# A fused attention and gated convolution: another table of issue order, engines and store queues

## The chip, the core and the metric

The kernel runs on one core of a Trainium2 chip. A core has TensorE (PE: matmuls and transposes, results into PSUM), VectorE (DVE), ScalarE (ACT) and GpSimd (POOL), each with its own queue that it works through in order, and SyncE (SP), which here only issues DMAs. DMAs can be issued by SP, ACT and POOL. PSUM has eight banks of 128 partitions x 512 fp32 values. The metric is the time of one execution on the device in microseconds (us); less is better.

## The reference

Two softmax attentions with 32 packed queries between them, then a gate whose middle factor is a circular convolution along the sequence:

```python
def sm_attn(qq, kk, vv):
    a = softmax(qq @ kk.T / sqrt(64)); return a @ vv
p_packed = sm_attn(p, k, v)                  # 32 x 64 for each of 8 x 8 heads
x = sm_attn(q, p_packed, p_packed)           # 576 x 64 for each, heads side by side: 8 x 576 x 512
x1, x2, x3 = split(x @ w_proj)               # each 8 x 576 x 512
x2 = irfft(rfft(x2, axis=1) * rfft(filter))  # along the 576 places
out = (x1 * x2 * x3) @ w_out                 # 8 x 576 x 512, fp32
```

## The kernel before, in words

The eight batches go one after the other through four stages, and the stages of neighbouring batches lie side by side in time. `front(b)` turns p, k and q (on PE, or by a DMA transpose where `TURNED` or `KEYS` names the batch), makes the first softmax with its sums on PE (`pv`), its reciprocal on DVE (`rz`), the packed values, their transpose, its copies into a block tile (`ppk`), the scores of the second softmax and its probabilities `a`. `turn(b)` projects the packed values with `wp` (`qm`), brings the probabilities to the frequency domain (`fa`, by way of `ez`) and turns them (`a2t`). `middle(b)` multiplies five spectra with the filter's (`tt`, `gm`, on DVE and POOL) and makes the gate x1 * x3 in four quarters and a rest (`w`; a copy of x1 out of PSUM, then a multiplication by x3). `back(b)` makes the inverse transform (`y`, `yt`) and the product with `wout`, copies it on ACT into the same quarters of `w` (or into `os`), and stores it: six stores a batch, eight where the rest of two batches goes with it.

Buffers: two each of k, v, q (`kn`, `vn`, `qn`; even and odd batches) and of `w`. So batch b + 2 can be loaded when PE has read batch b, and batch b + 2's gate copy into a quarter of `w` waits until batch b's store out of that quarter has landed.

Nothing of the order on the engines is set by the program's text. A recorder (`Recorder`) takes down every operation in the order of the text, with the engines that could do it (`either`), and then `emit` issues them in the order of a table, with the engine and the PSUM bank that the table names, each tied to the one before it on its engine. The table is `TABLE`, three numbers for each operation and one for each PSUM tile, packed. Since all operations are issued from one line of `emit`, the trace gives the same line, L193, for all; tiles tell them apart.

All loads of p, k, q, v, `wp` and `wout` are issued by POOL, between its arithmetic. The stores go through `send`, which lets the table choose SP or ACT. The DMA transposes are SP's.

Last, `spin(n)` records n matmuls of 256 columns on a tile of zeros, whose results are not read. The table places them among PE's work: 59, of which 39 stand ahead of the first real matmul.

Of the kernel before, what the change touches and what calls it, by code (L numbers as in the profile page):

```python
# [18 lines left out]
P = 128  # L19
# [29 lines left out]
def _constants(S):  # L49
# [34 lines left out]


TABLE = (
    'c-qaD30zdw8o=+pbMK5x;8TfQMiEUgL(NLfEtQ^<h+FtGOM0nKd%2eQs+Y~&1=j$>P*cOSMGec;lw8QALJ1_rB|*((kr)LH(3hA#@qOnz=g!<2%pBbM&'
    'vLi3eEWB!@8hqD*XoP4e6CsAT?@JLuwdq|1_xgZ;;&q2)vBW9?}5Oj7A;y_2q2to?xL(2q10-1R5WRFzNpmi?5X0@CrcbzCBDbXYZuijIC7*Z;)~=g%S'
    '}IVp#0#%!(yGRL;Ke3Z-|s2KD+m17VpVL(&{tz&#XkYto|(@IgCtNb+nj~QC9Y1Ou@Miel-wp8*;S7O9u5j-QN+ha(GdnzWq-PEzBF7H0b!ifr}#|p3G'
    '$&Wn9>=@0|_oE!_7&_IJUVK|yDc-KD^Gy5{DFryDeAkY0c1hI$2rpDMQD@!0zH8`lBHzF=goUHcOuGxInh=5S$Q&Mqg3IiF=_#*9TK%p8RDK~h$RA(6e'  # L90
    'dZcR<?^XSpmJ9eZz7`Sm`z{<3=W{Veh-mrXm(!yTI+O<6?pD*sqSnw$NubI6b(wgBrMVil;FyYN;|6var2oI|l=q3IqPd@BtZQuT<#>bmIAd2_jAJnuB'
    'qi)^Gv|tZ5HLYY^v|4{-oGnCndT<;k=0C<W4xiY8lpQHA{~6h|3dt(``4`}^qWtaI*}04NrT?&>@x|V~oA>TtgREP(>x&es?`p<Zb5<tRe|PCdLek8)k'
    'oaYUm2uNfAj=Y|cfLpVZ_SS}@W#7@@v{h%rp3n2QD1Q)Z=Eq?$-H?lha@D}V#C5zH7rciLT3*4l0LrA0)HR=$Rlk#Mn;DAZQVMeLx*mG9sIh4HF$v`MD'
    'ZQ1*5GFuQb4owk*B*g{k2g=?b0&8$2>S`Vzh0Wclf)DCuqb41Y}T~W@eUd$vh7v?@T+si-w`&gSF{f!jT@jY2ywe-H~rMBYTh>WY?z6Takc|kmN6s<x7'
    '+2uR|7H+BA!iuxi!PPYom)nKvtEiI)sxbQ%&xczfX7@Rp1rp@e1w#y|BuA$`mgl39<w&~^OamiVYm_a}kpM+83i^wXWY{0o>ogwgedkdUAOqZxjq7z4U'
    '8#Nocd!Bx-nI0Lk+)4Z+&DCm3jYB0z1G!gueN_v=CQPIe!yxgbG<;%jkU6qwZb&>L%oK4?<FMZ}D{|FaCz~Z_+XnhqSH8uIl-v|f(muKM2NiR9b?Oe%7'
    '>Em#`v|{|WsZ*2ksgLvWei)gazVO6529nkyi)O!v^!Ue$6`?B<6O(5709yN@gBL7_nKjYL+p)1PPeVE&EhkT${^}b@{_NQgAtT4p)QgS|_|K?O<6f*gp'
    'n`$!i|Sb$8Qx{h<3k-~NW0=rotBk!4`b+srnny|Ed>VrMaFYY?kC0i>O`)Vgchvg7cg?tfMI3i|LyH(3w}3{x3SVoUfsx;K79itg|X(-$&**FpEz;$gz'
    'Zi~!rHX?xdGAJ2y<5y7A6pWK0x$IoV#uQ>h}rSht}!H;`y(w9Ko2fe0lii{pUm?CN<pmaXU@eH_H1a{yR2SoA1HcvG2T|Fpe>3P)vIyYVep41Cv8TJB='
    '7IY#20=z|OsTIqJ3R1Uz)PO_$*2%^!ZyYHdq;_9OnCyD@y~Fz8!AW6~h6HC{v8e#6z&E<$Bx?F*E1z**7=OB|)eMr&tX@{-+*^Q4M=z4Oe{?T$0=QNvC'  # L100
    '>Nt<rU(VX0zEy%~&V@@-sIT)YB5jIUN$csmgt615`B+Pg-N>9LN-kJ0sW5S%-fRdn$Swv8P2ci>(R|Umu$dVBw<o-^kOnH4M&~IvF<UkV0g9cU%oj5U{'
    'R`$r;-blA-LZ7bIen`iN34~swix~fOGW>XZ1Fd_9cu6b&tBfXr_cdztJ9iH8-{Whw_V3Xn$MIxQkzegYNIOx?pmF^1r2~qAS;;cuJO8WIDq=nQ5|S|Xb'
    '!2&bUS71xq`WdJi$ObL>ZJ0?E0C|hNoG8OW?a;B9?1e)U_SY3K`Ux(>a~S45L!-VOhQ_Zr}N&7qNOA{@ik;z5F?yco8YmbR>oMy^D3?|CaU2`q<`q>P9'
    '8i>ib%(&!rL_l+BEOpyvjh+TD^PU=kG_N@7fbm-@dKSW7`PrSsD>Ba%6ZH65#ZOXfREO7BnUE8uq4zD7Vphh7U4R@<&$D<gk*S`D-3cnhiemEu<{j^`3'
    'a}GLU*vB(FRb99MV>xKeV$fiFF$a^^91S5+nc!r1*^EH2x=EE-)}`o4j6$v^)1<ENXDaUW(KIFvni8zXDazRVvEtvFb`D|_d+`_l4L_X3Bv9y&xGewVZ'
    '5$lfLUGQQ5r&dyAu%|9zWC39y+M%p(S8M}9+r+*7?0;&QZKvClr_>i-Ba#Zl3kbG0vPydfMoRd-bgJpD7@+Ft50atXgbK`B*7`@eJ{0VW&?IBM8k0T%a'
    'dLmb!C0}<SE)o|f$2rB5<r^$=V`SYR?gnK?RW};5t*X1gXl2!N3B}{+y6@%-&G<~yRBzE>5zQr$dmPA~o2za*dqjkrzOw3}2r;nxQnEs;AbBFI<l}rIJ'
    'FjqryA1G5wyQF86}zVkLR$#v<i;Q9a2?>OW=sU?FmJ8ua+2(dEf7)$-E^5`4R1OxRn@N9;ZL<Ic6+rQ?Z$JvOgn6h^FC}~$35*}8JRvL=WJYzE)E;cZn'
    '{~OT3TTzF)mjS7opMdOp|pKeG<dNOJ2vKE3%j;^xgH$B%9-jO;f2Xiqq0e0=$%~`9d}Xk0-btF+4!h!Hy@em`4=pj+14wJN{%lY^vWS7up}#L)ODpW&!'
    'I_D!ew8=2r3`ury*MXYk{0ZyC^)cuNm9n1rcMl+`eoHIGbi>V-l(jbUT9h9&gv=t?qL5Z9wQr%#PhHTHm5I>uhDk<e(j8*nOWQ}DiGb0wj1oZZGQ-F>d'  # L110
    'uy)~#)D7*bS<(-zO>TLmB?pZ!i7z|8y?F?W;;wY|!gGjUMIj7oW)w3<LU{Q=0y8RWmX!B@-G!`|xhK|+P;Oq5q=0+;H9_5NN|20E;%G8VQeZgMSM8~j@'
    'vF&Jz(;Ry8XwFl6wLGDEXoj-IN`_G~&DBe(E%ZCM5i~uUUVS~IpH>&$z=~{>NzI{lu^H_HiRNZ6O|2Heq^uio75tmUWiM>@y8B75P;JB%Hd3qTO`D#u7'
    '*|G|w$$Urrh49?Wm2}gcLYUs1)Td6h<@W6qAGjzQMU{-MxV1=dpwpEkE5%GI^Qj>`>N%VN<V@sZu*mXGR;mr*ArfkErZM4lEbbGX;<7u(ns5ME253{Ca'
    'V_{4-+^eOV!nMhM2(#p0A-YS;wu@8lJjc+#a}_g2ylXcs$ks{-$r<a20^NgYcd*@!p7b;~D%d>d)VPU2C`rf2Tyc9k%$R0O9Y{hPPtk>jvAs@IejIiob'
    'yn)t7Tmj+*7dtvJCY5zl*N=(~}WcetwEgW~e1%k%ubtRZ|&dQWxXZ?@#~cfaQFciqQ#G_dY@g50tZ_`jrF{9nX6H81P@U3xXFY1s0&t8??WGLFBkUb>~'
    '#cu5pElf?`l(PTE8M2nd>nJt3AiExzQlC$s<FPJ5ZD4GP$BJiTfixxrREGD=iaApgcz)L1cgt72UFq=476P6@P@D@=L%)DfgM3@W{OcD$=n*~V{C5aOx'
    '6EDE#l0bHWEkur7!XycXz`BANHZ{Ri3uod?usMw7%o1-F1Q;v{oCNyAEKamYW|IXL<Sj4(gfk1EhlvM;1hZ%{@jToy@k}sS943n(6KDxa31+hda+)n12'
    'ZMRoLo^d%M9IwYpeX!-U>q!O22oA0um}PPU=1_R31*@Ps18Pfjld?b5g1kg$zYNNq_tRhGbqi8f(YvKu(ip|;ao`qX<-}QWCB;f@us60G^2=MH{}1{Jm'
    '1;'
)  # L120


# [77 lines left out]
def kernel(  # L200
# [11 lines left out]
    nc = Recorder(tc)  # L212
    B, H, S, D = q.shape
# [24 lines left out]
    def pst(shape, dtype=FP32):  # L238
        return nc.psum(banks, shape, dtype)
# [390 lines left out]
    def spin(n):  # L630
        still = rings[2].rearrange("p h c -> p (h c)")
        for _ in range(n):
            o = pst([P, 2 * P])
            nc.tensor.matmul(o, still[:, 0:P], still[:, 0:2 * P], start=True, stop=True)
# [21 lines left out]
    for b in range(B):  # L656
# [3 lines left out]
        turn(b)  # L660
        middle(b)
        back(b)
    spin(59)
    nc.emit()


# [28 lines left out]
```

## Time and profile before

| | before |
|---|---|
| time, median of 3 runs | 188.88 us (186.68 to 193.44) |
| the profiled execution | 186.75 us, span 185.0 us |
| PE busy | 95% of the span |
| DVE, POOL, ACT busy | 82%, 72%, 68% |
| granted clock of PE | 0.996 of full speed |
| DMA | 32.98 MB, mean 178 GB/s |

The span runs from the first to the last recorded instruction of the core; about 1.75 us of the execution lie outside it. A matmul's record covers its way through the array, and the next one starts before it ends, so PE's busy share says when PE stood without any work, not how well it is used.

### The profile page before, as it was taken

What the parts mean: (1) busy time and instruction counts of PE and PEld (TensorE: products, weight loads), DVE (VectorE), ACT (ScalarE), POOL (GpSimd) and SP (SyncE); (2) the same over time, 40 slices, a digit from 0 to 9 for tenths busy, and PEclk for the clock granted to TensorE, in tenths of its full rate; (3) what the DMA queues carried; (4) which work ended last, traced back from release to release, by engine and by line L of the source; (5) the groups of instructions that cost most, each with busy time, mean ns of one, the idle gap of its engine ahead of it and who ended that gap; (6) DMA issues with size and microseconds to landing.
All of it is one profiled execution on the core that took longest, in us unless ns stands there. A gap on an engine that the chain in (4) does not pass through costs nothing.

```text
span 185.0 us, 5942 instructions
## 1 busy us (share of the span) xinstructions
PE 175.0 (95%) x2439; PEld 116.7 (63%) x2439; DVE 151.2 (82%) x276; ACT 126.1 (68%) x282; POOL 133.8 (72%) x117
## 2 busy tenths in 40 slices
PE   6979969999999999999999999999999999999990
PEld 4646636658855696466676665567577884585840
DVE  5152799998996889989999889769999998986840
ACT  2385886798785997888967666879788756225241
POOL 7493407999989945699797986967399989689000
PEclk9999999999999999999999999999999999999998
DMA  5999999999999999999997999995999503512625
GB/s 173 284 196 206 196 200 196 248 198 164 174 180 201 221 223 192 156 244 226 197 147 121 257 169 249 178 124 72 223 208 243 193 4 68 169 60 73 211 105 182
DMA packets 51243, 32.98 MB, mean 178 GB/s; under 512 B 21456, under 2 KB 46032, under 8 KB 51216
## 3 DMA queue, kind: packets, MB, share of 16 engines
q0 software_dynamic: 27280, 16.52, 63.3%
q1 hardware_dynamic: 22384, 13.01, 31.6%
q10 hardware_dynamic: 1552, 3.06, 5.4%
q8 instruction: 19, 0.31, 0.7%
q14 instruction: 8, 0.07, 0.1%
HBM read 35.24 MB, written 9.44 MB: 242 GB/s over the span
## 4 chain that ended last, share of the span: by engine, by line
PE 71%; DMA 14%; ACT 5%; DVE 3%; issue 2%; POOL 2%; POOLq 0%; ACTq 0%
PE ps L193 71%; DMA qn<-in_q_dram 5%; DMA pn<-in_p_dram 5%; DMA out_dram<-w 4%; ACT qm L193 1%; POOL a L193 1%; ACT a L193 1%; DVE w L193 1%; ACT e L193 1%; DVE zs L193 1%; DVE qT L193 1%; ACT ez L193 1%; POOL wout L193 0%; ACT w L193 0%; ACT wt L193 0%
## 5 line engine op out<-in xcount | busy, mean ns | idle before, releaser
L193 POOL TENSOR_TENSOR tt<-tt,tt 128x1024 f32<-128x1024 f32 (+1 forms) x20 | 38.2, 1925 | 8.7 <-DVE tt L193 7.5
L193 POOL TENSOR_TENSOR gm<-tt,tt 128x512 f16<-128x512 f32 x32 | 40.0, 1274 | 0.6
L193 PE MATMUL ps<-a2t,qm 128*128 128x128 f16 (+2 forms) x352 | 39.3, 253 | 0.0
L193 DVE TENSOR_TENSOR tt<-ps,h 128x1024 f32<-128x1024 f32 x32 | 37.8, 1215 | 0.9 <-PE ps L193 0.5
L193 PE MATMUL ps<-wout,y 128*128 128x512 f16 x128 | 33.0, 379 | 0.1
L193 PE MATMUL ps<-ac,gm 128*128 128x288 f16 (+2 forms) x288 | 30.0, 246 | 0.0
L193 PEld LDWEIGHTS <-qm 128*128 128x128 f16 x352 | 22.6, 98 | 9.7 <-issue 0.4
L193 ACT ACTIVATE w<-ps 128x512 f32<-128x512 f32 x32 | 18.4, 599 | 12.8 <-PE ps L193 12.4
L193 DVE TENSOR_TENSOR w<-w,ps 128x512 f32<-128x512 f32 (+1 forms) x40 | 24.4, 625 | 1.6 <-ACT e L193 1.3
L193 PEld LDWEIGHTS <-gm 128*128 128x128 f16 x288 | 21.3, 98 | 4.6 <-issue 0.2
L193 DVE SCALAR_TENSOR_TENSOR y<-w,ps 128x512 f16<-128x512 f32 (+2 forms) x36 | 21.1, 620 | 2.9 <-PE ps L193 2.4
L193 PE MATMUL ps<-qm,fa 128*128 128x512 f16 x80 | 22.8, 380 | 0.0
L193 ACT COPY w<-ps 128x512 f32<-128x512 f32 (+1 forms) x27 | 15.1, 571 | 10.4 <-PE ps L193 7.1
L193 POOL TENSOR_TENSOR a<-a,zr 128x1152 f16<-128x1152 f16 x7 | 14.9, 2127 | 9.5 <-DVE zr L193 4.5
L193 ACT CAST qm<-ps 128x512 f16<-128x512 f32 x35 | 19.4, 594 | 3.3 <-PE ps L193 3.2
L193 PEld LDWEIGHTS <-y 128*128 128x128 f16 x128 | 11.5, 98 | 11.3 <-issue 1.0
L193 PEld LDWEIGHTS <-a 128*128 128x128 f16 x210 | 13.5, 98 | 7.7 <-ACT qm L193 2.0
L193 ACT ACTIVATE e<-ps 96x384 f16<-96x384 f32 x32 | 14.4, 489 | 5.4 <-PE ps L193 5.2
L193 PE MATMUL ps<-iw,a 128*128 128x64 f16 (+2 forms) x178 | 16.7, 229 | 0.0
L193 POOL TENSOR_TENSOR fa<-ez 128x256 f16<-128x256 f32 x12 | 8.6, 729 | 9.2 <-DVE ez L193 5.6
L193 POOL DMA_DIRECT2D qn<-in_q_dram x16 | 12.4, 780 | 2.5 <-DMA vn<-in_v_dram 1.9
L193 PEld LDWEIGHTS <-ppk 64*32 64x32 f16 (+1 forms) x267 | 8.9, 95 | 7.4 <-issue 2.1
(80 smaller groups left out, 297.2 us busy)
## 6 DMA issues: line engine op xcount, KB each, us to landing
out_dram<-w SPq DMA_DIRECT2D x20, 256.0 KB, 4.8
vn<-in_v_dram POOLq DMA_DIRECT2D x8, 576.0 KB, 10.6
qn<-in_q_dram POOLq DMA_DIRECT2D x8, 512.0 KB, 10.5
kn<-in_k_dram POOLq DMA_DIRECT2D x7, 576.0 KB, 11.3
wp<-in_moe_w_proj_dram POOLq DMA_DIRECT2D x4, 256.0 KB, 13.1
out_dram<-w ACTq DMA_DIRECT2D x4, 256.0 KB, 5.0
out_dram<-w SPq DMA_DIRECT2D x6, 128.0 KB, 4.9
out_dram<-w SPq DMA_DIRECT2D x10, 64.0 KB, 2.9
```

The source lines that it names most:

```text
L193: ins = getattr(self.real[engine], what)(*args, **kw).ins
```

## The change

The table is another one: for the same operations it names other places in the order, for 105 of them another engine (81 of arithmetic and copies between ACT, DVE and POOL; 24 stores between SP and ACT: 13 go from ACT to SP, 11 from SP to ACT), and other PSUM banks. Of the 118 DMAs SP issues 62 (60 before), ACT 15 (17), POOL 41 (41). Besides, there are eight fillers more, and 32 instead of 39 stand ahead of the first real matmul. No operation is added or taken away otherwise.

```diff
@@ -84,39 +84,39 @@
 TABLE = (
-    'c-qaD30zdw8o=+pbMK5x;8TfQMiEUgL(NLfEtQ^<h+FtGOM0nKd%2eQs+Y~&1=j$>P*cOSMGec;lw8QALJ1_rB|*((kr)LH(3hA#@qOnz=g!<2%pBbM&'
...
+    'c-qaG30M`?9>DLJxib@q0%66&Kr{uB%%D#~Ef-S5O2ssbr=g~nxtA@zF0))L#lXri#RV**!W9=Z;6p?ccQ&7vAc`O+8X`Ot1r^`fX71bzB$%ncd$}{`%'
...
 )
@@ -660,7 +660,7 @@
         back(b)
-    spin(59)
+    spin(67)
     nc.emit()
```

Three places of the new order follow, each as it was and as it is. First POOL's queue from the loads of batch 1 to its first work on the spectra of batch 0 (`kn_79`, `qn_83`, `vn_81` are the buffers of odd batches, `kn_78`, `qn_82` of even ones), before:

```order
L193 DMA vn_81<-in_v_dram 96x8x384
L193 DMA qn_83<-in_q_dram 128x1x256
L193 TENSOR_TENSOR fa_111<-ez_113 128x2x128
L193 DMA kn_78<-in_k_dram 96x8x384
L193 TENSOR_TENSOR fa_111<-ez_113 128x2x128
L193 DMA qn_82<-in_q_dram 128x1x256
L193 DMA qn_82<-in_q_dram 128x8x256
L193 DMA kn_79<-in_k_dram 96x8x384
L193 TENSOR_TENSOR tt_122<-tt_121,tt_122 128x512 x2
```

and in the new order:

```order
L193 DMA qn_83<-in_q_dram 128x1x256
L193 DMA qn_83<-in_q_dram 128x8x256
L193 DMA vn_81<-in_v_dram 96x8x384
L193 DMA kn_78<-in_k_dram 96x8x384
L193 DMA qn_82<-in_q_dram 128x8x256
L193 DMA qn_82<-in_q_dram 128x1x256
L193 DMA kn_79<-in_k_dram 96x8x384
L193 ISA
L193 TENSOR_TENSOR tt_122<-tt_121,tt_122 128x512 x2
```

The two operations on `fa` have gone to DVE, and no arithmetic of POOL stands among these loads any more. The second place is POOL's queue right behind its eight operations on the spectra of batch 0, before:

```order
L193 DMA qn_83<-in_q_dram 128x1x256
L193 DMA vn_80<-in_v_dram 96x8x384
L193 TENSOR_TENSOR a_104<-a_104,zr_108 128x1152
L193 DMA wout<-in_moe_w_out_dram 128x4x512
L193 DMA qn_83<-in_q_dram 128x8x256
```

and in the new order:

```order
L193 DMA vn_80<-in_v_dram 96x8x384
L193 DMA wout<-in_moe_w_out_dram 128x4x512
L193 TENSOR_TENSOR a_104<-a_104,zr_108 128x1152
L193 DMA qn_83<-in_q_dram 128x8x256
L193 DMA kn_78<-in_k_dram 96x8x384
```

The load of `wout` now stands ahead of the normalisation of batch 1's probabilities, and the small load of q further back. The third place is SP's queue from the transpose of batch 5's q to that of batch 6's q (`w_118` holds batch 2, `w_119` and `os` batch 1, `kn_78` batch 6), before:

```order
L193 DMA_TRANSPOSE qT_95<-qn_83 128x18x128
L193 DMA_TRANSPOSE kT_93<-kn_78 128x6x96
L193 DMA_TRANSPOSE kT_89<-kn_78 128x6x96
L193 DMA out_dram<-w_119 128x512
L193 DMA out_dram<-os 64x512
L193 DMA out_dram<-w_118 64x512
L193 DMA_TRANSPOSE kT_91<-kn_78 128x6x96
L193 DMA_TRANSPOSE kT_90<-kn_78 128x6x96
L193 DMA out_dram<-w_118 128x512 x2
L193 DMA_TRANSPOSE qT_94<-qn_82 128x18x128
```

and in the new order:

```order
L193 DMA_TRANSPOSE qT_95<-qn_83 128x18x128
L193 DMA_TRANSPOSE kT_91<-kn_78 128x6x96
L193 DMA_TRANSPOSE kT_90<-kn_78 128x6x96
L193 DMA_TRANSPOSE kT_93<-kn_78 128x6x96
L193 DMA_TRANSPOSE kT_89<-kn_78 128x6x96
L193 DMA out_dram<-w_118 32x512
L193 DMA out_dram<-os 64x512
L193 DMA out_dram<-w_118 128x512
L193 DMA out_dram<-w_118 64x512
L193 DMA out_dram<-w_118 32x512
L193 DMA out_dram<-w_118 128x512 x2
L193 DMA_TRANSPOSE qT_94<-qn_82 128x18x128
```

The four transposes of batch 6's k now stand together, and all six stores of batch 2 behind them on this one queue, where ACT issued three of them before.

The fillers behind the first real matmul stand, on PE: one ahead of the transpose of batch 0's p (two before), five from there to the sums of batch 0's softmax (one before), 22 from there to the spectra of batch 0 (17 before), and seven ahead of batch 1's scores (none before).

## Rows read from the trace of the kernel before

**Rows 1.** Two lines of the page: busy time by engine, and the last chain.

```profile
PE 175.0 (95%) x2439; PEld 116.7 (63%) x2439; DVE 151.2 (82%) x276; ACT 126.1 (68%) x282; POOL 133.8 (72%) x117
PE 71%; DMA 14%; ACT 5%; DVE 3%; issue 2%; POOL 2%; POOLq 0%; ACTq 0%
```

**Rows 2.** Table by stretches: length, busy time by engine, PE's clock, DMA share, GB/s.

```profile
0.00:12.00 12.00, 8.89 (x52) 6.03 (x53) 4.40 (x17) 4.82 (x9) 8.44 (x15) 1.00 0.98 220
12.00:30.00 18.00, 16.25 (x252) 10.05 (x251) 12.85 (x28) 12.52 (x27) 6.38 (x9) 1.00 1.40 199
30.00:50.00 20.00, 19.95 (x350) 14.93 (x349) 19.11 (x33) 16.54 (x43) 19.38 (x20) 1.00 1.28 198
50.00:70.00 20.00, 19.94 (x345) 13.18 (x342) 17.30 (x33) 16.77 (x38) 16.05 (x13) 1.00 1.27 205
70.00:90.00 20.00, 20.00 (x273) 12.23 (x271) 18.52 (x33) 17.08 (x39) 16.81 (x15) 1.00 1.26 204
...
110.00:130.00 20.00, 19.58 (x271) 11.87 (x269) 16.61 (x29) 15.48 (x37) 14.36 (x11) 1.00 1.09 159
```

**Rows 3.** Timeline of PE: start, duration, operation, idle before.

```profile
10.45 0.23 PE L193 MATMUL ps<-iw,pn 128*128 128x128 f16 x1 [1.45 <-DMA pn<-in_p_dram]
...
21.87 0.94 PE L193 MATMUL ps<-ppk 128*128 128x256 f16 x7
...
27.02 0.38 PE L193 MATMUL ps<-wt,a 128*128 128x512 f16 x1 [1.72 <-ACT qm L193]
```

**Rows 4.** The last chain in order of time: start, duration, what.

```profile
48.06 9.78 DMA qn<-in_q_dram
...
107.38 7.76 DMA out_dram<-w
```

**Rows 5.** Timeline of POOL, its 15th and 16th load.

```profile
21.20 0.78 POOL L193 DMA_DIRECT2D vn<-in_v_dram  x1 [2.21 <-DMA wp<-in_moe_w_proj_dram]
22.50 0.62 POOL L193 DMA_DIRECT2D qn<-in_q_dram  x1 [0.52 <-DMA wp<-in_moe_w_proj_dram]
```

**Rows 6.** Timeline of POOL, ahead of and behind batch 0's spectra.

```profile
28.76 0.72 POOL L193 TENSOR_TENSOR fa<-ez 128x256 f16<-128x256 f32 x1 [5.64 <-DVE ez L193]
29.44 0.81 POOL L193 DMA_DIRECT2D kn<-in_k_dram  x1
...
47.24 0.82 POOL L193 DMA_DIRECT2D wout<-in_moe_w_out_dram  x1
```

**Rows 7.** Table by stretches, two short ones.

```profile
45.00:46.00 1.00, 1.00 (x16) 0.95 (x15) 0.48 (x3) 0.59 (x2) 0.83 (x1) 1.00 1.03 107
...
54.00:56.00 2.00, 2.00 (x44) 1.01 (x27) 2.00 (x3) 1.13 (x3) 2.00 (x1) 1.00 1.39 195
```

**Rows 8.** Timeline of DVE, ahead of batch 0's reciprocal.

```profile
12.07 0.68 DVE L193 TENSOR_TENSOR gm<-os,gm 64x512 f16<-64x512 f32 x1 [0.68 <-ACT gm L193]
...
17.16 0.46 DVE L193 COPY kT<-ps 128x576 f16<-128x576 f16 x1 [3.75 <-ACT tt L193]
```

**Rows 9.** DMA issues: KB each, median to landing; whole span, then 156 to 176 us.

```profile
out_dram<-w SPq DMA_DIRECT2D x20, 256.0 KB, 4.8
...
out_dram<-w ACTq DMA_DIRECT2D x4, 256.0 KB, 5.0
...
out_dram<-w SPq DMA_DIRECT2D x5, 256.0 KB, 2.4
```

**Rows 10.** Timeline of SP, transposes and stores of batches 1 to 6.

```profile
95.87 2.51 SPq L193 DMA_TRANSPOSE kT<-kn  x2
...
105.30 2.78 SPq L193 DMA_DIRECT2D out_dram<-w  x2
115.80 3.57 SPq L193 DMA_TRANSPOSE qT<-qn  x1
```

**Rows 11.** Timeline of ACT, around the gate of batch 4.

```profile
110.85 1.56 ACT L193 CAST qm<-ps 128x512 f16<-128x512 f32 x3 [1.03 <-PE ps L193]
...
115.21 0.58 ACT L193 COPY w<-ps 128x512 f32<-128x512 f32 x1 [1.82 <-DMA out_dram<-w]
```

## The prediction before the run

> **What bounds the kernel now.** I read the page first: TensorE is busy for 95% of the span, and 71% of the chain that ended last is its matmuls [rows 1]. The next view is the table by stretches [rows 2], and the reader should take 100% minus PE's busy share from each line. From 0 to 12 us PE is idle for 3.11 us, from 12 to 30 for 1.75, from 30 to 50 for 0.05, from 50 to 70 for 0.06, from 110 to 130 for 0.42; from 70 to 90, as from 90 to 110 and from 130 to 150, it is idle for nothing. So behind 30 us PE runs almost without a gap until its last matmul, and an order of issue can win there only what the small gaps hold, about 0.6 us.
>
> The timeline of PE [rows 3] says what the early gaps are: 1.45 us for the first load of p, and 1.72 us for a cast of ACT. Between the first matmuls and there, PE also runs fillers, matmuls on a tile of zeros whose result nobody reads (`spin`). Seven in a row take 0.94 us, of which 0.27 is the length of the last, so one costs (0.94 - 0.27) / 6 = 0.11 us of PE's time. Of the 59, 39 stand before the first real matmul and 20 behind it: 2.2 us.
>
> That gives a ceiling. The time before the filter's first matmul and the wait for p are set by loads that go first before and after. All other idle time and all later fillers together are 1.75 + 0.6 + 2.2 = 4.5 us. The work itself, the same instructions, can't shrink. To be faster by 2% (3.7 us) the new order would have to remove four fifths of all that is left.
>
> The chain in order of time [rows 4] names the two things outside PE that touch it late: a load of q that lands just when PE asks for it (issued at 48.06, 9.78 us), and a store of 7.76 us, issued at 107.38, for which ACT waits, and PE behind ACT.
>
> **Fillers.** The profiled execution took 186.75 us for a span of 185.0, and I make the sum against that. In the new order 32 fillers stand first and 35 later, so 15 more stand where they can cost something: 1.65 us in all. By place: one fewer ahead of the wait for p, which absorbs it, 0. Four more between p and the sums of batch 0's softmax, 0.44; this stretch holds next to none of PE's 1.75 us of waits, so I take half, 0.22 (bounds 0 and 0.44). Five more between those sums and batch 0's spectra; there the row shows the wait of 1.72 us, which swallows their 0.55, so 0; without that cover they cost 0.55. Seven in batch 1, ahead of its scores, 0.77: the table shows no wait there (0.05 in the whole stretch from 30 to 50), so they count in full (bounds 0, if a wait has moved there, and 0.77). Sum: +0.99. The seven fillers fewer at the start cost nothing: the first real matmul waits for a loaded table and a cast, not for them.
>
> **Loads.** POOL issues its transfers in order with its arithmetic, and it may have eight in flight: its 15th, a load of v, waits for the 7th, a load of wp, and its 16th for the 8th, another of wp, 1.30 us later [rows 5]. In the old order POOL stands idle for 5.64 us until 28.76 for an input of fa and issues k of batch 2 only behind that, at 29.44 [rows 6]. In the new order nothing stands between; k of batch 2 is the 17th and goes out when the 9th has landed, one such step later, at about 23.8, 5.6 us earlier. What hides most of this: the transfers wait in line anyway. What is left is a dip: from 45 to 46 us the DMA moves 107 GB/s, from 54 to 56 it moves 195 [rows 7], so 0.45 us of transfer is lost in this slice, and neighbours bring it to about 1 us. It stands where POOL has just done its eight additions and subtractions of batch 0 and issued no load. They remain where they were, since their inputs do; but wout, at 47.24 before [rows 6], now goes ahead of the wait for batch 1's softmax, some 3 us earlier. So the load of q that landed at 57.84 has a lead of 1 to 3 us, and the gap at PE there (0.06 in the whole stretch, [rows 2]) goes: -0.06. The late piece is then v of batch 2, which PE now wants about 2 us sooner than before; I see its landing just ahead of it, 0 (bounds 0 and +1).
>
> **Batch 0's own chain.** Of batch 0 and the filter eight copies move from ACT to DVE, eight back, and three operations of POOL to DVE. Ahead of batch 0's reciprocal DVE gets one subtraction more, which POOL did (0.68 for the like of it), and copies for such as it loses. It had 3.75 us of idle time before 17.16 [rows 8], which covers this: 0.2 (bounds 0, and 1.0 when the cover is gone). What could be won here is at most the wait of 1.72.
>
> **Stores.** 24 transfers, all stores, change between SP's queue and ACT's: 13 go to SP, 11 to ACT. The queue as such is free: the 256 KB stores land 4.8 us after issue on SP, 5.0 on ACT [rows 9]. What counts is what stands ahead of them. On SP the old order has two transposes of batch 6's k, a store of batch 1, and then the stores of batch 2 between and behind the other transposes. The new one has all four transposes first (2.51 us for two, so 5.0 from 95.87 on), then six stores of batch 2 and one of batch 1, and then the transpose of q that waits for its load until 115.80 [rows 10]. The store on which ACT waited 1.82 us at 115.21 [rows 11] was issued by ACT at 107.38 behind other work; on SP it can go at about 102 and has landed by 110. That takes the 0.42 away. But the store of the quarter that PE finishes last can't go out before about 107.7, where it went before (the second of the row at 105.30), and the copy that overwrites its slot, on DVE before, now stands on ACT right behind three casts that ended at 112.4 [rows 11]. At 4.8 us the store has landed at 112.5; at 7.76 it lands at 115.5 and ACT waits 3. I take -0.2 for both together (bounds -0.42 and +3).
>
> **Sum.** 186.75 + 0.99 - 0.06 + 0.2 - 0.2 = 187.7. On the median of the runs shown, 188.88, the same +0.93 gives 189.8. Two of the four executions known stand at 186.7 and the others above, for which the trace has no reason, so I lean to the first: 188.2. All else (81 of some 630 instructions of ACT, DVE and POOL change their engine, as many in one direction as in the other, and most others shift by a few places) I put at 0: DVE is idle for 18% of the span and the others for more [rows 1].
>
> **Rivals.**
> The first ends slower: stores that share one queue. Alone, at the end, a 256 KB store lands in 2.4 us; beside loads it takes 4.8 [rows 9], and 7.76 where several stand together [rows 4]. With batch 2's stores on one queue in a row, behind four transposes, each can come later by the length of the one before, and ACT, which works in order, stands before each of batch 4's four gate copies; behind it wait the casts and exponentials that PE needs. Place: 110 to 120 us, and again at batch 6, where three stores of batch 4 now follow four others. Price: 3 us for the first place by the bound above, and half of it for the second, where fewer loads run: 186.75 + 0.99 + 3 = 190.7 with the first place alone and 192.2 with both, 191.5 as its middle. It decides from the point where the last store of batch 2 lands later than 112.4. For it speaks the wait that the old order has there already, against it that the very store which held ACT there now goes out earlier. The Trainium skill has a rule for this (DMA: Bandwidth & Descriptors, section on queues, rings and completion order): each DMA engine takes turns between the queues that have work. By that, stores on two queues beside the loads would have two turns of three and on one queue one of two, so an estimate from that page's rule and the 7.76 row is 10.3 us instead of 7.76, and 5.6 us of waiting for ACT. The equal medians on SP and ACT neither bear that out nor rule it out, since both were measured beside each other.
>
> The second ends faster: the fillers all lie in waits, batch 0's chain gets shorter and the wait of 1.72 goes with the 0.42 and the 0.06: 186.75 - 2.2 = 184.55. For it: DVE idles 3.75 us ahead of that chain. Against it: DVE gets more to do there and more fillers stand there, not fewer. It would be 1.2%, and only with a share of the older fillers over 2%.
>
> The third: the change doesn't do what it says. POOL is free 5.6 us earlier, but the transfers wait for buffers or stand in line, the moved stores meet nobody, the new fillers lie in waits; the time is that of before, 186.7 to 188.9.
>
> **How the numbers follow.** Forecast 0.58 (187 to 189.8), the first rival 0.18, the second 0.11, the third 0.13. The range reaches from half of the second rival, 185.2 (its own 184.55 is given up with the 2 in 10), to the middle of the first, 191.5. Faster by over 2% takes nearly everything in the ceiling, so 0.08; slower by over 2% is the first rival, 0.17; within 2% is the rest, 0.75. Two per cent is also about what a measurement of this kernel can tell from no change.
>
> **What would show it.** In the new profile k of batch 2 should be issued at about 24, the DMA's rate between 44 and 47 should not fall as low, and PE should have no gap at 57.8. PE should run seven fillers at about 40 and no more idle time than before between 30 and 110. ACT's wait for a store near 115 should be shorter than 1.82 or have moved to the gate copy behind three casts. The prediction is wrong if PE's idle time behind 30 us exceeds 2 us (an input I took as covered), or if the first 30 us change by more than 1 us.

## The result, and the profile after

The changed kernel takes 189.12 us (median of 22 executions, 187.31 to 192.43), the kernel before 188.66 beside it (22 executions, 185.67 to 194.68). The ratio is 1.0084, with a 95% interval of 1.0056 to 1.0112: slower by 0.8%, 1.6 us, within the 2% of "no change"; the medians differ by 0.46 us. Executions of both kernels spread over several us; ratios here leave out the long ones, medians do not, and the profile of the changed kernel that follows is a long one (192.43 us, span 190.7). No execution of it near 189 us was profiled, so what such a one loses is read from E2 to E10.

The first line is the page's busy time, with the share of the span, of the changed kernel. It answers to [rows 1]: PE was busy for 2.9 us more than before, and idle for 12.8 of 190.7 us.

```profile
PE 177.9 (93%) x2447; PEld 117.1 (61%) x2447; DVE 149.7 (79%) x275; ACT 128.2 (67%) x282; POOL 134.1 (70%) x118
```

The table by stretches of the changed kernel says where; its columns are those of [rows 2], and its lines answer to them.

```profile
0.00:12.00 12.00, 9.33 (x62) 6.03 (x63) 4.62 (x16) 5.58 (x9) 7.63 (x14) 1.00 0.96 218
12.00:30.00 18.00, 17.11 (x257) 10.12 (x254) 13.89 (x33) 12.86 (x28) 7.09 (x9) 1.00 1.40 198
30.00:50.00 20.00, 19.83 (x362) 15.43 (x359) 19.03 (x33) 17.00 (x43) 17.75 (x17) 1.00 1.32 211
50.00:70.00 20.00, 20.00 (x349) 13.37 (x346) 17.84 (x35) 15.68 (x34) 15.88 (x13) 1.00 1.16 171
70.00:90.00 20.00, 20.00 (x265) 11.84 (x263) 18.29 (x33) 17.51 (x39) 17.81 (x16) 1.00 1.27 215
110.00:130.00 20.00, 15.63 (x202) 8.50 (x201) 10.50 (x19) 10.40 (x25) 10.85 (x8) 0.83 0.91 159
```

Up to 30 us PE's idle time fell from 4.86 to 3.56 us. From 110 to 130 us it rose from 0.42 to 4.37, and there the granted clock was 0.83. The timelines of SP, POOL, ACT and PE of the changed kernel around that place:

```profile
98.09 5.67 SPq L193 DMA_TRANSPOSE kT<-kn  x4
103.86 1.59 SPq L193 DMA_DIRECT2D out_dram<-w  x1
105.50 0.49 SPq L193 DMA_DIRECT2D out_dram<-os  x1
106.09 5.57 SPq L193 DMA_DIRECT2D out_dram<-w  x5
...
103.15 0.83 POOL L193 DMA_DIRECT2D vn<-in_v_dram  x1
105.90 0.79 POOL L193 DMA_DIRECT2D kn<-in_k_dram  x1
...
109.38 0.26 ACT L193 COPY ppk<-ps 64x128 f16<-64x128 f16 x1 [0.35 <-PE ps L193]
115.05 0.58 ACT L193 COPY w<-ps 128x512 f32<-128x512 f32 x1 [5.41 <-DMA out_dram<-w]
115.65 0.53 ACT L193 COPY ppk<-ps 64x128 f16<-64x128 f16 x2
...
110.04 1.82 PE L193 MATMUL ps<-ac,gm 128*128 128x288 f16 x24
116.23 1.30 PE L193 MATMUL ps<-wp,ppk 64*32 64x512 f16 x16 [4.37 <-ACT ppk L193]
```

These answer to [rows 10] and [rows 11]. The first of the five stores in a row, at 106.09, is batch 2's second quarter of `w` (`project_out(3)`). Batch 4's gate copy into that quarter (`gate(1)`) waited for it for 5.41 us; two copies of `ppk` stood behind it on ACT, and PE waited 4.37 us for them. In the kernel before the same copy waited for the same store, for 1.82 us, and PE for 0.42. The store itself landed no later than before: at 114.95 us (below), and at 107.38 + 7.76 = 115.14 in [rows 4]. What moved is the copy. Its start less its wait is when ACT came to it: 115.05 - 5.41 = 109.64 us, against 115.21 - 1.82 = 113.39 in [rows 11]. The new table puts this gate ahead of batch 5's projection; in the kernel before it stood behind it, so that all copies of `ppk`, here in ACT's timeline of the kernel before, were long done:

```profile
108.99 0.83 ACT L193 COPY ppk<-ps 64x128 f16<-64x128 f16 x3
```

So the slot was asked for 3.75 us sooner and came free 0.2 us sooner, and other work that PE needs stood behind the copy. The chain of the changed kernel in order of time shows the store with its landing; it answers to the second line of [rows 4].

```profile
106.09 8.86 DMA out_dram<-w
...
115.05 0.09 ACT w L193
...
115.65 0.26 ACT ppk L193
...
116.23 17.21 PE ps L193 x216
```

The clock fell within the wait, near 114 us, when PE had stood for 2 us, and stayed low behind it. The column ahead of the last two is the granted clock, of the changed kernel in three slices of 2 us:

```profile
116.00:118.00 2.00, 1.77 (x18) 0.52 (x19) 1.76 (x4) 1.03 (x3) 0.00 (x0) 0.50 1.35 223
118.00:120.00 2.00, 2.00 (x7) 0.63 (x6) 2.00 (x3) 1.27 (x3) 0.16 (x1) 0.50 1.06 139
122.00:124.00 2.00, 2.00 (x19) 1.06 (x18) 0.67 (x3) 1.98 (x6) 1.92 (x3) 1.00 1.02 228
```

0.50 is the lower of the two levels, 1.2 GHz. The six matmuls of 512 columns on `a2t` there took 2.74 us; in the run E11, without the fall, the same six took 1.46.

The early steps, in POOL's and PE's timelines of the changed kernel, and the DMA's rate from 45 to 46 us, answer to [rows 3], [rows 6] and [rows 7]:

```profile
24.69 0.77 POOL L193 DMA_DIRECT2D kn<-in_k_dram  x1 [0.85 <-DMA wp<-in_moe_w_proj_dram]
43.06 0.79 POOL L193 DMA_DIRECT2D wout<-in_moe_w_out_dram  x1
...
25.73 0.22 PE L193 MATMUL ps<-iw,a 128*128 128x128 f16 x1 [0.52 <-DVE a L193]
39.35 0.93 PE L193 MATMUL ps<-ppk 128*128 128x256 f16 x7
...
38.89 1.07 ACT L193 COPY ppk<-ps 64x128 f16<-64x128 f16 x4
...
45.00:46.00 1.00, 1.00 (x27) 1.00 (x25) 1.00 (x3) 0.72 (x3) 1.00 (x1) 1.00 1.21 172
```

### The profile page after: what moved, and what is told of

The parts are those of the page before. It is cut to its first block, busy times and chain, and to the rows that moved or that the text cites. A ratio compares the mean times of both kernels' runs of the same rounds, so it can differ in the third digit from the quotient of the medians.

```text
span 190.7 us, 5941 instructions
## 1 busy us (share of the span) xinstructions
PE 177.9 (93%) x2447; PEld 117.1 (61%) x2447; DVE 149.7 (79%) x275; ACT 128.2 (67%) x282; POOL 134.1 (70%) x118
## 4 chain that ended last, share of the span: by engine, by line
PE 73%; DMA 20%; POOL 2%; ACT 2%; issue 1%; ACTq 0%; POOLq 0%
PE ps L193 73%; DMA wp<-in_moe_w_proj_dram 8%; DMA qn<-in_q_dram 7%; DMA out_dram<-w 5%; POOL qn L193 1%; POOL kn L193 1%; POOL pn L193 0%; POOL vn L193 0%; ACT qTm L193 0%; ACT os L193 0%; ACT ppk L193 0%; ACT a L193 0%; ACT ez L193 0%; ACT a2t L193 0%; ACT w L193 0%
## 5 line engine op out<-in xcount | busy, mean ns | idle before, releaser
L193 PE MATMUL ps<-a2t,qm 128*128 128x128 f16 (+3 forms) x352 | 41.1, 258 | 0.0
L193 PE MATMUL ps<-wout,y 128*128 128x512 f16 x128 | 32.2, 379 | 0.0
L193 PE MATMUL ps<-ac,gm 128*128 128x224 f16 (+2 forms) x288 | 29.4, 246 | 0.0
L193 ACT COPY w<-ps 128x512 f32<-128x512 f32 (+1 forms) x34 | 18.3, 558 | 16.3 <-PE ps L193 5.7
L193 PE MATMUL ps<-qm,fa 128*128 128x512 f16 x80 | 23.6, 386 | 0.0
L193 ACT CAST qm<-ps 128x512 f16<-128x512 f32 x33 | 18.7, 592 | 5.4 <-PE ps L193 5.2
L193 PE MATMUL ps<-iw,a 128*128 128x64 f16 (+2 forms) x178 | 17.6, 229 | 0.5 <-DVE a L193 0.5
L193 POOL TENSOR_TENSOR fa<-ez 128x256 f16<-128x256 f32 x14 | 10.0, 732 | 5.5 <-ACT ez L193 5.4
## 6 DMA issues: line engine op xcount, KB each, us to landing
qn<-in_q_dram POOLq DMA_DIRECT2D x8, 512.0 KB, 12.8
```

What stands on the lines that cost most here:

```text
L193: ins = getattr(self.real[engine], what)(*args, **kw).ins
```

## The experiments

Each run is the changed kernel (E8: the kernel before) with a few rows of its table moved. The last four columns are of each run's own profile: PE's idle time in two stretches, the granted clock of the second, the span.

| run | median (range, n), us | before beside it | ratio (95%) | idle 70 to 90 | idle 110 to 130 | clock | span |
|---|---|---|---|---|---|---|---|
| before | | | | 0 | 0.42 | 1.00 | 185.0 |
| changed | 189.12 (187.31 to 192.43, 22) | 188.66 | 1.0084 (1.0056 to 1.0112) | 0 | 4.37 | 0.83 | 190.7 |
| E1 | 193.48 (190.02 to 194.19, 4) | 188.29 | none | 0.22 | 4.45 | 0.83 | 191.6 |
| E2 | 188.74 (187.48 to 191.11, 10) | 188.29 | 1.0070 (1.0023 to 1.0117) | 2.83 | 0 | 1.00 | 187.2 |
| E3 | 190.00 (187.52 to 192.15, 4) | 188.29 | none | 2.04 | 0.97 | 1.00 | 187.5 |
| E4 | 188.88 (187.15 to 193.16, 10) | 188.29 | 1.0062 (1.0011 to 1.0113) | 0.70 | 4.13 | 0.83 | 191.3 |
| E5 | 190.28 (188.56 to 192.02, 5) | 190.33 | 1.0123 (1.0023 to 1.0224) | 0 | 2.64 | 0.91 | 188.5 |
| E6 | 187.91 (187.04 to 190.24, 5) | 190.33 | 1.0012 (0.9904 to 1.0121) | 0 | 2.66 | 0.91 | 187.7 |
| E7 | 186.25 (185.76 to 186.78, 5) | 190.33 | 0.9928 (0.9860 to 0.9997) | 0.10 | 0.37 | 1.00 | 184.9 |
| E9 | 187.12 (186.03 to 192.96, 10) | 191.71 | 0.9979 (0.9909 to 1.0048) | 0 | 0.44 | 1.00 | 184.3 |
| E10 | 187.23 (185.61 to 189.84, 10) | 191.71 | 0.9991 (0.9940 to 1.0043) | 0.15 | 1.25 | 1.00 | 185.3 |
| E11 | 186.42 (185.48 to 187.52, 12) | 191.71 | 0.9960 (0.9914 to 1.0007) | 0.29 | 0.85 | 1.00 | 184.6 |
| E12 | 186.01 (185.28 to 189.28, 12) | 191.71 | 0.9946 (0.9891 to 1.0001) | 0.06 | 0.07 | 1.00 | 184.4 |

E8 has a median of 190.84 (186.42 to 192.23, 5; before 190.33) and no ratio.

**E1 to E4: is it this store, or the fillers, or the early order?** The theory A: the late store. The rivals: B, the fillers; C, the first 30 us.

E1 is the changed kernel again.

> The changed kernel once more, unchanged, for a second profile of it. Theory A (a store of batch 2 that leaves SP late holds ACT's gate copy of batch 4, and PE behind it): the wait of PE near 112 us is there in every execution, from about 1.5 us in the quickest to the 4.4 us of the first profile, and its length sets the time. Theory B (the fillers cost the 0.99 us of the sum, the wait of 4.4 us is an accident of one execution): in a quick execution PE does not wait near 112 us and the time still is 1 us above that of the kernel before. Theory C (the first 30 us got longer): PE's idle time up to 30 us is 1 us or more above the 4.86 us of before.

Its profile has the wait (4.45 us) and PE idle for 2.87 us up to 30 us (before 4.86): C falls. That the wait is there in every execution, and B in a quick one, it can't tell: the profiled execution took 193.34 us, and the quickest, 190.02, was not profiled.

E2 moves one store on SP's queue:

```diff
 DMA_TRANSPOSE kT_93<-kn_78
+DMA out_dram<-w_118 128x512
 DMA_TRANSPOSE kT_89<-kn_78
 DMA out_dram<-w_118 32x512
 DMA out_dram<-os 64x512
-DMA out_dram<-w_118 128x512
```

> One transfer of the changed kernel moved on SP's queue: batch 2's store of the second quarter of w goes out one DMA transpose earlier, as soon as ACT has filled the quarter (99.85 us), ahead of three other stores instead of behind two. It should go out near 102 to 103 and land near 108 to 111, where the gate copy wants the slot at 109.6. Theory A: PE's wait near 112 us goes to under 1 us, the time falls by 1.5 to 2 us against the changed kernel, to 187 to 187.6, ratio to before 0.995 to 1.0. Theory B or C: no change, ratio to before stays at 1.006 to 1.011. A third outcome: the next store in the row (the first quarter's or the last one's) takes over the wait, and half of the gain is lost.

The store went out at 103.22 and landed at 105.97, and from 110 to 130 us PE did not wait at all. Yet the ratio stayed at 1.007, which theory A did not allow: this execution lost 2.83 us from 70 to 90 us instead. The chain in order of time of E2 names that second place:

```profile
74.51 7.35 DMA out_dram<-w
...
81.94 0.59 ACT w L193
...
82.58 5.87 PE ps L193 x144
```

It is the same pattern one batch pair earlier. Batch 0's store of the first quarter, filled by ACT at about 63 us, stands on SP behind the DMA transpose of batch 4's q, which holds SP's queue from 67.27 for 7.19 us. It stood there before too, at the head of the five stores in SP's timeline of the kernel before:

```profile
67.26 4.80 SPq L193 DMA_TRANSPOSE qT<-qn  x1
72.17 4.25 SPq L193 DMA_DIRECT2D out_dram<-w  x5
```

But batch 2's gate copy into that quarter came last of the four then, on DVE, at 83.27. The change moved it to the second place, on ACT, in front of work that PE needs; in the changed kernel's profile it ran at 78.64.

E3 takes the seven fillers ahead of batch 1's scores out (seven matmuls on PE, with their weight loads).

> The seven fillers ahead of batch 1's scores taken out of the changed kernel, nothing else. By the sum of the prediction they cost 0.77 us in full: the time falls by 0.77, ratio to before 1.004. Rival: in the profile of the changed kernel they run from 39.35 to 40.12 us, while ACT copies the block tile that the scores read until 39.96, so most of them lies in a wait: the time falls by 0.1 to 0.2 us, which is less than can be told, and the ratio stays at 1.008.

PE's timeline of E3 shows in their place a wait for the same copies that the fillers had stood beside:

```profile
40.24 0.39 PE L193 MATMUL ps<-ppk,qT 128*128 128x64 f16 x8 [0.50 <-ACT ppk L193]
```

Its idle time from 30 to 50 us is 0.68 us, against 0.17 in the changed kernel: in this execution 0.5 of the 0.77 us of the seven fillers lay in a wait. The total can't be read from four executions; this profile lost at both places (2.04 and 0.97).

E4 moves the held copy on ACT behind the two `ppk` copies:

```diff
-COPY ppk_88<-ps_64
+COPY ppk_88<-ps_64 x3
 COPY w_118<-ps_67
-COPY ppk_88<-ps_64 x2
```

> The held gate copy of batch 4 moved on ACT behind the two copies of the block tile that stood behind it and that PE waits for; nothing else is moved. If theory A holds and ACT's order alone hands the wait on, PE's wait near 112 us shrinks by 1 us or more and the time falls by as much (187.5 to 188). If the PSUM bank that the copy holds hands it on too (the projection of batch 5 writes the same bank), PE stands in front of the second matmul of that projection instead, and the time stays within 0.4 us of the changed kernel's. Theory B or C: no change either, but then also no wait of PE at this place in a quick execution.

PE's timeline of E4:

```profile
111.96 0.39 PE L193 MATMUL ps<-wp,ppk 64*32 64x512 f16 x1
116.47 1.05 PE L193 MATMUL ps<-wp,ppk 64*32 64x512 f16 x15 [4.13 <-ACT w L193]
```

PE got through one matmul more and then stood for 4.13 us: the second one writes the bank that the held copy has still to read. The wait is handed on by the bank as well as by ACT's order, so this later place on ACT does not cure it; the slot has to come free earlier, or the gate has to come later on PE too.

**E5 to E8: two places, or one limit?** E5 moves batch 0's store ahead of the transpose, on SP:

```diff
 DMA out_dram<-w_118 128x512
+DMA out_dram<-w_118 128x512
 DMA out_dram<-w_118 32x512
...
 DMA_TRANSPOSE qT_94<-qn_82
-DMA out_dram<-w_118 128x512
```

> One transfer of the changed kernel moved on SP's queue, at the earlier of the two places where a store holds ACT: batch 0's store of the first quarter of w, filled at 62.94 us, goes out ahead of the DMA transpose of batch 4's q (which holds SP's queue from 66 to 73.4 us) instead of behind it. The later place, batch 2's store of the second quarter, is left as it is. Theory A2 (the transfers alone set when the slot at the later place comes free, 115 us; PE either waits 2 to 2.8 us near 80 us and little there, or not near 80 us and over 4 us there, with the clock falling behind it): PE's wait near 80 us is gone in every execution, the one near 112 us is 4 us or more in every execution, and the time rises to 190 to 193. Rival A1 (the two waits are independent losses): 2 us come back, 186.5 to 187.5.

The time did not fall by 2 us, as A1 wanted; the median is 190.28, the ratio 1.0123, not told from the changed kernel's 1.0084, and the profile has nothing left near 80 us and this at the later place:

```profile
114.55 1.14 PE L193 MATMUL ps<-wp,ppk 64*32 64x512 f16 x16 [2.64 <-ACT ppk L193]
```

A2 was right that nothing comes back; its size, 4 us or more in every execution, was too large. So a wait near 80 us had partly paid for itself. E3 and E5 show how: the store landed at 113.0 us in E3 (6.9 us behind its issue at 106.13) and at 113.3 in E5 (7.7 behind 105.55), but ACT came to the copy at 111.74 in E3, which had waited near 80 us, and at 109.69 in E5, which had not. PE's delay also moved POOL's work, and with it the load of v of batch 6: to 106.44 and 105.25 us in E2 and E3, against 103.15 to 103.32 in the changed kernel, E1 and E5. E9 and E10 show why the place of this load matters too.

E6 makes both moves.

> Both stores moved, batch 0's first quarter ahead of the transpose of batch 4's q, batch 2's second quarter ahead of the last transpose of batch 6's k; two transfers on one queue, nothing else. Theory A2 and A1 alike: neither wait is left; the profile with the second store alone moved had a span of 187.2 with 2.8 us of PE's waits between 70 and 90 us and none from 110 to 130, so 184.4 to 184.8, a time of 186.2 to 186.6, and hardly an execution above 189. Ratio to before 0.992 to 0.998. Rival D (another store takes over at once, or the loss was in the first 30 us or in the fillers): 187.5 or more.

The median fell, to 187.91, less far than either theory had it: rival D, another store takes over. The copy that E2 freed does not wait any more; the next one does, for batch 2's first quarter, which went out at 108.75 and landed at 116.73. PE's timeline of E6:

```profile
117.46 1.01 PE L193 MATMUL ps<-a2t,qm 128*128 128x512 f16 x2 [2.66 <-ACT w L193]
```

E7 is E6 without 16 fillers (16 matmuls of `ppk` on PE, with their weight loads).

> As the one with both stores moved, and besides it 16 fillers are taken out: four between batch 0's p and its sums, five between the sums and the spectra, seven ahead of batch 1's scores. By the sum of the prediction these cost 0.99 us, so the time would be 185.2 to 185.6. Rival: they lie in waits, as the profile without the seven shows (PE idle 0.68 us between 30 and 50 us instead of 0.08): no more than 0.3 us below the one with both stores moved.

186.25, all five executions within 1.1 us. But PE did not get to the place sooner: the gate copy that E2 freed ran at 110.40, in E6 at 109.31. The store that the next copy waits for landed 1.3 us sooner, so that this wait cost PE 0.30 us instead of 2.66. Whether this was the fillers' own time is what E11 and E12 were made to tell.

E8 moves the store in the kernel before, on ACT:

```diff
 ACTIVATE w_118<-ps_62
+DMA out_dram<-w_118 128x512
 DMA out_dram<-w_118 32x512
...
 COPY qTm_97<-qT_95 x2
-DMA out_dram<-w_118 128x512
```

> The kernel before with one transfer moved on ACT's queue: batch 2's store of the second quarter, filled at 101.14 us, goes out near 102.1 instead of 107.38 us. Theory A: the copy that waited 1.82 us there does not wait, PE's 0.42 us near 115 go, and if the long executions of the kernel before (190 to 194 us) come from the same wait grown to 4 us, they become rare: the median falls from 188.3 to about 187. Rival: the long executions have another place; the median stays and only some 0.4 us go.

No gain, as the rival had it. The copy of batch 4 did not wait for a store any more, but ACT's and PE's timelines of E8 show that the kernel before can have this kind of wait too, one batch earlier: a gate copy of batch 3 waits for a store of batch 1.

```profile
107.21 0.58 ACT L193 COPY w<-ps 128x512 f32<-128x512 f32 x1 [4.25 <-DMA out_dram<-w]
...
108.12 1.03 PE L193 MATMUL ps<-qm,fa 128*128 128x512 f16 x2 [3.70 <-ACT fa L193]
```

That store went out at 99.03 and took 8.08 us; POOL had issued the load of v at 97.48.

**E9 to E12: what makes a store take 2 us or 9.** In the profiles of the changed kernel and of E1 to E7, batch 2's stores were sorted by whether they went out ahead of POOL's load of v of batch 6 or behind it (576 KB in the rows; the expectation's 1.18 MB is wrong). Ahead of it they had landed after 1.8 to 4.1 us, behind it, but for one (2.0 in E7), after 6.3 to 9.5. The change had moved this load: before it stands behind one operation on `gm`, now behind three and the normalisation, at 103.15, just ahead of batch 2's stores. POOL's timeline of the kernel before:

```profile
98.15 0.81 POOL L193 DMA_DIRECT2D vn<-in_v_dram  x1
```

That is theory E; rival F is that SP's queue alone makes the store late.

E9 puts the load back (with E5's store):

```diff
 TENSOR_TENSOR gm_117
+DMA vn_80<-in_v_dram
 TENSOR_TENSOR gm_117
 TENSOR_TENSOR a_103<-a_103,zr_107
-TENSOR_TENSOR gm_117
-DMA vn_80<-in_v_dram
-TENSOR_TENSOR gm_117
+TENSOR_TENSOR gm_117 x2
```

> Batch 0's store moved as in the run with that store alone, and besides it one load on POOL's queue put back where the kernel before has it: v of batch 6 (1.18 MB) goes out behind the first of the four operations on gm, near 97.6 us, instead of behind the third, at 103.2. SP's queue near 100 to 112 us is that of the changed kernel. Theory E (what decides how long a store takes is whether a large load was issued just ahead of it: in eight profiles batch 2's stores that went out ahead of v landed after 1.8 to 4.4 us, those that went out up to 5 us behind it after 6.2 to 9.5): v has landed near 106 to 107, the store of the second quarter, issued near 105.6 behind it, lands near 110 to 112 (only k, issued 0.3 us later, is beside it), PE's wait near 112 us falls from 2.6 to 4.4 us to under 1.5, and the time from 190.3 to 187 to 188.5. Rival F (SP's queue alone makes the store late, by its place behind the transposes): the store lands at 113 or later, no change of the time.

E10 does the opposite:

```diff
 TENSOR_TENSOR gm_117
-DMA vn_80<-in_v_dram
 TENSOR_TENSOR gm_117
 TENSOR_TENSOR fa_111<-ez_113
-DMA kn_79<-in_k_dram
 TENSOR_TENSOR fa_111<-ez_113
+DMA vn_80<-in_v_dram
+DMA kn_79<-in_k_dram
```

> The opposite: v of batch 6 and k of batch 7 are moved back on POOL's queue, behind the second operation on fa, to 106.7 and 107.5 us; batch 0's store moved as before, SP's queue as in the changed kernel. Theory E: the store of the second quarter, issued near 105.6, lands in 2 to 4.4 us, by 110, and ACT's gate copy into this quarter waits for less than 0.5 us; the store of the first quarter, issued near 108.7 behind both loads, takes 7 us or more and holds the next gate copy, so that PE's wait moves from 112 to about 115 us and is 1 to 3 us long; the time is 187.5 to 190. Rival F: the store lands at 113 or later and PE waits near 112 us as before.

The issue rows say how long the second-quarter store took, its last column, each in a slice that holds it alone: first E5, then E9, then E10. SP's queue has the same order in all three.

```profile
out_dram<-w SPq DMA_DIRECT2D x1, 256.0 KB, 7.7
```
```profile
out_dram<-w SPq DMA_DIRECT2D x1, 256.0 KB, 6.5
```
```profile
out_dram<-w SPq DMA_DIRECT2D x1, 256.0 KB, 4.1
```

POOL's timeline of E10, and ACT's of E9 (one line) and E10:

```profile
106.22 0.83 POOL L193 DMA_DIRECT2D vn<-in_v_dram  x1
```
```profile
110.60 0.59 ACT L193 COPY w<-ps 128x512 f32<-128x512 f32 x1 [1.30 <-DMA out_dram<-w]
```
```profile
109.93 0.59 ACT L193 COPY w<-ps 128x512 f32<-128x512 f32 x1 [0.21 <-PE ps L193]
115.95 0.59 ACT L193 COPY w<-ps 128x512 f32<-128x512 f32 x1 [2.05 <-DMA out_dram<-w]
```

In E9 the store went out at 104.02, with v already on its way for 7 us, and landed at 110.50, 2.8 us sooner than in E5; 1.5 of that is that it went out sooner. Batch 2's stores still took 5.9 to 7.7 us there, with the load of k of batch 7 issued among them at 104.71: an early v alone does not bring the short landings. In E10 it went out at 103.77, ahead of both loads, landed at 107.83, and the copy had no store to wait for; the first-quarter store, issued at 107.54 behind them, took 8.3 us and held the next copy, as expected. F falls: both loads are on POOL, and SP's order was left alone. That SP's order counts as well is shown by E2, where the store went out one transpose sooner, ahead of the load, and took 2.7 us. Both runs come to the time of the kernel before (0.998 and 0.999).

E11 makes E6's two moves and E9's, and lets batch 2's first-quarter store pass two others:

```diff
 DMA out_dram<-w_118 64x512
+DMA out_dram<-w_118 128x512 x2
 DMA out_dram<-w_118 32x512
-DMA out_dram<-w_118 128x512 x2
```

> Batch 0's store and batch 2's second-quarter store moved ahead as in the run with both, v of batch 6 put back as in the kernel before, and on SP the store of batch 2's first quarter goes ahead of two others (a part of the rest and the last quarter). Theory E: no gate copy of batch 4 waits for more than 0.5 us, PE has no wait over 0.5 us behind 30 us, the span is 184 to 184.8, the time 185.8 to 186.6 in nearly every execution, ratio to before 0.990 to 0.997. Rival: another store, of batch 1 or 3, takes over; 187.5 or more.

E12 is E11 without the 16 fillers.

> The same without the 16 fillers (four between batch 0's p and its sums, five to the spectra, seven ahead of batch 1's scores). With the stores out of the way this shows what the fillers cost: by the sum of the prediction 0.99 us less than the run with all four moved; by the rival reading (they lie in waits) 0 to 0.25 us less.

E11 has no execution above 187.52; a copy still waited 1.66 us for a store there (expected: below 0.5) and PE 0.78. E12 is 0.41 us below it, with 12 executions of each spread over 2 us and more: between the two readings, and by the times nothing that can be told from either. The traces tell more. ACT's copy that E2 freed, in E11 and in E12, and the longest of PE's waits of E12 between 12 us and there:

```profile
109.64 0.59 ACT L193 COPY w<-ps 128x512 f32<-128x512 f32 x1 [0.21 <-PE ps L193]
```
```profile
110.36 0.58 ACT L193 COPY w<-ps 128x512 f32<-128x512 f32 x1 [0.21 <-PE ps L193]
```
```profile
70.06 0.33 PE L193 MATMUL ps<-iw,a 128*128 128x128 f16 x3 [0.84 <-issue]
```

Without the 16 fillers this execution came to the place 0.72 us later, not sooner: from 12 to 70 us PE was idle for 2.62 us instead of 0.64, about as much more as the 16 fillers cost by the sum of the prediction (1.76 us). What it gained lies behind, where the next copy waited 0.56 us for its store instead of 1.66. E7 and E6 show the same pattern. So in these profiles the fillers' time lay in waits, as the rival reading had it.

E7, E11 and E12 are the quickest of all, 0.4 to 0.7% below the kernel before by their ratios, with intervals that end just below 1 for E7 and just above it for the other two.

## Why the prediction was wrong

**The failing step is "so I lean to the first: 188.2".** The sum said +0.93 us; measured were +1.6 by the ratio, +0.46 by the medians. Leaning to the two quickest of four known executions of the old kernel turned a forecast of slower by half a per cent into a number below the old median. The 22 executions of the kernel before that were measured beside the changed one don't stand at two places: they spread from 185.67 to 194.68. The sum should have been put on the median as it stood, 189.8. That this comes within 0.7 us of the 189.12 measured would have been luck all the same, since two of its terms were wrong in opposite directions: the fillers (+0.99) lay largely in waits, and the stores (-0.2) cost what the sum gave to the fillers.

**Stores: the term of -0.2 was mis-sized, and its reading was wrong in three places.** The prediction let the second-quarter store go out at about 102 and land by 110. It went out at 106.09 and landed at 114.95: the four transposes on SP began at 98.09, not 95.87, and ended at 103.8, two stores ahead of it held SP until 106, and then it took 8.86 us where the prediction had allowed about 8. Most of the delay is thus SP's queue, which the prediction read too early. The second place is the copy: ACT came to it at 109.64 instead of 113.39, an order that falls under "all else", which the prediction put at 0. A store that lands at 114.95 would have held a copy at the old place for 1.56 us, less than before. No run puts this gate back to its old place, so that its share is read from the two profiles, not shown by an experiment. So the wait that was thought gone (0.42 of PE) is the one that grew to 4.37 in the profile, and the copy that was named instead, for the first quarter, came next in line only where the first was cured (E6, E10). The third place, batch 0's store behind a transpose, was not seen at all: the diff moved its gate copy from DVE to ACT, ahead of work that PE wants (2.45 us in E2). With the store's move of E5 and POOL's loads moved, the ratio is 0.998 (E9) and 0.999 (E10), with intervals that end below that of the changed kernel, 1.0056 to 1.0112: the loss lies in these waits. Of the two signs of being wrong that the prediction named, both came: PE idle for over 2 us behind 30 us (4.37 in one wait), and a change of over 1 us up to there (1.30 less).

**Of a step that is moved its DMAs count: the load of v of batch 6 was left out.** The prediction read POOL's loads up to 50 us and none at 98. That load moved by 5 us, and where the loads stand took the store from 7.7 us (E5) to 6.5 (E9) and 4.1 (E10).

**Rival 1 had the place and the pattern, and half of the cause.** Store, gate copy on ACT, PE behind it, from 110 to 120 us: right, at 0.18. Its price of 3 us for the first place is near the 2.64 of E5 and below the 4.37 of the changed kernel's profile. That several stores on one queue make each other late is not what made this one slow to land: with the queue as it was, its time went from 7.7 to 4.1 us when the loads went behind it. The queue made it late to go out. The estimate that went with the Trainium skill's rule (DMA: Bandwidth & Descriptors, section on queues, rings and completion order), that a DMA engine takes turns between the queues with work, was 10.3 us; batch 2's stores on the one queue took 7.4 to 9.3 in the changed kernel, and mostly landed with v or behind it (v at 112.99, the stores ahead of and at 106.09 in SP's order at 113.16 to 114.95).

**Fillers: +0.99 was too much.** The seven ahead of batch 1's scores do not count in full: about 0.5 of their 0.77 us lies in a wait for `ppk` (E3), which the table of before could not show, since in its order the projection stood there. By the times all 16 together gave 0.41 us (E11 to E12), not resolved from 0.25 nor from 0.99 by the spread; in the profiles their place was taken by waits.

**Loads were right.** k of batch 2 went out at 24.69 (forecast 23.8), the rate from 45 to 46 us was 172 GB/s instead of 107, `wout` went 4.2 us earlier (forecast 3), and from 50 to 70 us PE did not wait. As forecast, it was worth nothing more than the 0.06.

**Batch 0's chain:** +0.2 was forecast; the wait of 1.72 us became 0.52, so this went the other way, as the second rival had it. What the new order is worth without most of its store waits is seen nearest in E9: 0.998, not told from 1, with a span of 184.3 in the profile against 185.0.

## What to carry to other kernels

A buffer's store and the write that reuses it are one step: when a table moves either, ask first when the write comes to the slot (here 3.75 us sooner), then when the store's own queue lets it out, then which large loads any queue issues just ahead of it: in these runs stores took 1.8 to 4.1 us ahead of such a load and mostly 6.3 to 9.5 behind it, and moving the loads alone took one store from 7.7 us to 4.1. A copy that waits for such a store should not stand on an in-order engine, or in a PSUM bank, ahead of what TensorE needs next. And a sum made against one profiled execution belongs on the median as a difference; choosing a base afterwards turned its sign here.

## What was not expected of the hardware

In these profiles one long wait cost more than two shorter ones, and part of the difference is the clock. Behind PE's wait of 2.64 us in E5 the granted clock was 0.50, behind 2.45 us near 80 us in E2 it stayed at 1.00 (first E5, then E2):

```profile
116.00:118.00 2.00, 2.00 (x6) 0.76 (x5) 2.00 (x3) 1.27 (x3) 0.00 (x0) 0.50 1.45 196
```
```profile
82.00:84.00 2.00, 1.42 (x20) 0.92 (x20) 0.43 (x1) 2.00 (x5) 2.00 (x2) 1.00 1.18 285
```

The profiles of E2 and E3, which lost 2.8 and 3.0 us to these waits at full clock, are 3.2 to 4.4 us shorter than those of the changed kernel and E1, with 4.4 us in one. PE's shorter waiting is 1.4 to 1.8 us of that; the rest is put down to the stretch at 1.2 GHz, not shown by a run. Repairing one of two waits (E5) did not shorten the kernel: the copy at the second place came to its slot 2 us sooner than in E3, and the store landed no sooner. What decides whether an execution waits at the first place (0 in the changed kernel's profile, 2.83 in E2's, with the same order up to there), and how much of the spread of the kernel before comes from waits like E8's, was not settled.
